# The last unit's inverses and normalization, issued inside the first layer's steps

## The chip, the cores and the metric

The kernel runs on one core of a Trainium2 chip. The metric is the device time in microseconds (us) of one execution. The engines work side by side, each through its own list of instructions in order, and they meet at semaphores: TensorE (PE, its weight loads are PEld), VectorE (DVE), ScalarE (ACT), GpSimd (POOL), and SyncE (SP), which issues nearly all DMAs of this kernel.

## What is computed

Linear attention over 4 batches of 8 heads (576 positions, head size 64), then two feed-forward layers over the 2304 tokens. Cut to what matters:

```python
proj = x @ w_phi                               # for q and for k, 64 -> 128 features
proj = proj - max(abs(proj))                   # per row
phi = concat([exp(proj), exp(-proj)])
kv = phi(k).T @ v ; z = sum(phi(k))
num = phi(q) @ kv ; den = phi(q) @ z + 1e-6
attn = num / den                               # 32 heads -> x of 2304 x 512
h = x @ w_in1 ; x = (h * cos(h)) @ w_out1      # 512 -> 2048 -> 512
h = x @ w_in2 ; out = (max(h, 0) ** 2) @ w_out2
```

The feed-forward weights are float64. Every matmul of the two layers is made of three, of high and low halves.

## The kernel before

**Attention.** The heads are taken two at a time: 16 units, u = 0 to 15, four for each batch. A unit is cut into named steps, and a planner puts the steps of all units, of the first weight tiles' conversion and of the start of the first layer into one list (`keys`), which `emit` then issues one by one. Each engine carries out its own instructions in the order in which the list names them. The last steps of a unit are a chain over several engines. `C` copies numerators and denominators out of PSUM into the tile `tm` (ACT). `D1` reshapes the 2 x 576 denominators from `tm` into `cp` of 32 x 36 (two small DMAs on SP's queue). `I` adds 1e-6 and takes the reciprocal (two DVE instructions, L613 and L614). `D3` writes `cp` to `db` in DRAM, and `D4` reads it back, spread over 64 partitions a head, into `dn` (three DMAs on SP's queue). `Z0` and `Z1` multiply `tm` by `dn` into `xbuf`, the layers' input (two POOL instructions, L629).

**Feed-forward.** `feed_forward` goes through ten blocks j of tokens: j = 0 to 4 for the first layer (tokens 0 to 511, 512 to 767, then three blocks of 512), j = 5 to 9 for the second. A block has 16 chunks c of the hidden size. At step i of a block PE runs `G1(j, i)`, twelve matmuls (L289 to L291), and `G2(j, i - 3)`, twelve matmuls (L385) that use the result of `G1` three steps earlier. Between them stands the elementwise chain of a chunk: `A1` on ACT (L304, L305), `A2a` and `A2b` on DVE (L309, L311), `B1` on ACT (L314, L315), `B2` on DVE (L319), `B3` on ACT, which writes the high half of `g` (L324), and `B4` on DVE, which writes the low half (L327). Here g(c) is what `G2` of chunk c needs. There are two buffers for `tr` and two for `g`. `G1` of the chunks 0 to 3 of block 0, and parts of their elementwise work, are steps of the list `keys` and stand before `feed_forward`.

**Weights.** 32 tiles of the first layer are loaded as float64 and turned into two halves on the chip: three ACT instructions (L227, L229, L231), four on DVE or POOL (L242, L244, L246, L249), one on ACT (L255) and one more (L259). Tiles 0 to 19 are done in `keys`. Tiles 20 to 31 are converted on ACT and DVE inside block 0, about nine tiles in ten steps. Their loads are issued on SP's queue in two groups: tiles 20 to 28 (`wnext`, nine loads of 512 KB) when the attention's buffers are free, and tiles 29 to 31 (`wlast`, three loads) when `tm`, `cp` and `dn` are.

**The order at the seam.** The last lines of the kernel issue `keys` up to the last attention step that is not a tail step, then the nine `wnext` loads, then the rest of `keys`, then the three `wlast` loads, then `feed_forward`. The rest of `keys` holds, among the early elementwise steps of chunks 0 to 3, the tail of unit 15: `C01`, `C11`, `D1`, `I`, `D3`, `D4`, `Z0`, `Z1`. Unit 15 holds tokens 1728 to 2303, which the first layer reads in its blocks 3 and 4.

Of the kernel before, what the change touches and what calls it, by code (L numbers as in the profile page):

```python
# [158 lines left out]
def attention_ffn_kernel(  # L159
# [20 lines left out]
    NU = len(UNITS)  # L180
    NEARLY, NNEXT = 21, 9
# [5 lines left out]
    with tc.manual_schedule():  # L187
        const = ctx.enter_context(tc.tile_pool(name="const", bufs=1))
        pools_w = [ctx.enter_context(tc.tile_pool(name="wearly", bufs=1))]
# [18 lines left out]
        NTILE = len(order)  # L208
        weights, raw_t, mag_t = {}, {}, {}

        def w_slot(i, dtype, shape, name):
            pool = pools_w[(i >= NEARLY) + (i >= NEARLY + NNEXT)]
            return pool.tile(shape, dtype, tag=f"w{i}", name=name)

        def w_load(layer, n):
            part, c = order[n]
            s = w_slot(n + 1 - layer, I32, [P, KDM * P, 2], "raw")
            src = ((w_in1, w_out1), (w_in2, w_out2))[layer][part]
            nc.sync.dma_start(out=s.rearrange("p f t -> p (f t)"), in_=src.bitcast(I32)[c * P:(c + 1) * P, :])
            raw_t[layer, n] = s  # L220
# [49 lines left out]
        def split_x(j, kk, part):  # L270
            _, o, n = BLOCKS[j]
            src = xbuf[:, kk, o:o + n]
            x = work(XS[kk][part], [P, n], F32R, "xs")
            if part == 0:
                nc.scalar.activation(out=x, in_=src, func=ACTF.Copy)
                xs_t[kk] = (x,)
            else:
                hi = xs_t[kk][0]
                nc.vector.tensor_tensor(out=x, in0=src, in1=f(hi), op=ALU.subtract)
                xs_t[kk] = (hi, x)  # L280

        def G1(j, c):
            layer, _, n = BLOCKS[j]
            hps = bank(H_BANKS[c % 4], name="h")[:, 0:n]
            w = weights[layer, 0, c]
            ih, il = (w[:, i].rearrange("p (k f) -> p k f", k=KDM) for i in range(2))
            for kk in range(KDM):
                xh, xl = xs_t[kk]
                nc.tensor.matmul(out=hps, lhsT=ih[:, kk, :], rhs=xh, start=kk == 0, stop=False)  # L289
                nc.tensor.matmul(out=hps, lhsT=ih[:, kk, :], rhs=xl, start=False, stop=False)  # L290
                nc.tensor.matmul(out=hps, lhsT=il[:, kk, :], rhs=xh, start=False, stop=kk == KDM - 1)  # L291
            h_t[c] = hps
# [37 lines left out]
        def elementwise(j, i, conv):  # L330

            layer = BLOCKS[j][0]

            def a(name):
                if i < KFF:
                    part(name, j, i)

            def b(name):
                if 1 <= i <= KFF:
                    part(name, j, i - 1)  # L340

            if layer == 0:
                b("B1")
                conv(w_join, 0)
                a("A1")
                b("B2")
                conv(w_join, 1)
                a("A2a")
                conv(w_join, 2)
                conv(w_join, 3)  # L350
            else:
                conv(w_join, 0)
                a("A1")
                conv(w_join, 1)
                b("B1")
                conv(w_join, 2)
                conv(w_join, 3)
            b("B3")
            if layer == 0:
                a("A2b")  # L360
            conv(w_split, 0)
            b("B4")
            conv(w_split, 1)
            for step in range(3):
                conv(w_words, step)

        def G2(j, c):
            layer, _, n = BLOCKS[j]
            g = g_t.pop(c)
            gh, gl = g[:, 0], g[:, 1]  # L370
            w = weights[layer, 1, c]
            oh, ol = w[:, 0], w[:, 1]
            na = KDM if layer == 0 else n // P
            if c == 0:
                acc[:] = [bank(ACC_BANKS[m], name=f"acc{m}") for m in range(na)]
            for m in range(na):
                sl = slice(m * P, (m + 1) * P)
                if layer == 0:
                    trip = ((oh[:, sl], gh), (oh[:, sl], gl), (ol[:, sl], gh))
                    o = acc[m][:, 0:n]  # L380
                else:
                    trip = ((gh[:, sl], oh), (gl[:, sl], oh), (gh[:, sl], ol))
                    o = acc[m]
                for i, (l, r) in enumerate(trip):
                    nc.tensor.matmul(out=o, lhsT=l, rhs=r, start=c == 0 and i == 0, stop=c == KFF - 1 and i == 2)  # L385

        def evict(j):
            layer, o, n = BLOCKS[j]
            for m, a in enumerate(acc):
                if layer == 0:  # L390
                    dst, src = xbuf[:, m, o:o + n], a[:, 0:n]
                else:
                    dst, src = mag_p.tile([P, DM], F32, tag="mag", name="ot"), a
                if m % 2:
                    nc.scalar.activation(out=dst, in_=src, func=ACTF.Copy)
                else:
                    nc.vector.tensor_copy(dst, src)
                if layer == 1:
                    nc.sync.dma_start(out=out[o + m * P:o + (m + 1) * P, :], in_=dst)
# [4 lines left out]
        class Ticks:  # L404
# [16 lines left out]
            def share(self, rate):  # L421
                self.due += rate
                n = int(self.due)
                self.due -= n
                return [self.tick() for _ in range(n)]
# [12 lines left out]
        def retire(j, i):  # L438
            if j == LAST_0:
                for n, (p, c) in enumerate(order):  # L440
                    if c + LA * p == i:
                        w_load(1, n)

        def feed_forward():
            for j in range(len(BLOCKS)):
                for i in range(KFF + LA):
                    if i < KFF and ("G1", j, i) not in early:
                        G1(j, i)
                    now = share(j, i)
                    elementwise(j, i, now[0] if now else lambda fn, *a: None)  # L450
                    for conv in now[1:]:
                        for fn, *a in STAGES:
                            conv(fn, *a)
                    if i == KFF and j + 1 < len(BLOCKS):
                        for kk in range(KDM):
                            split_x(j + 1, kk, 0)
                            split_x(j + 1, kk, 1)
                    if i >= LA:
                        G2(j, i - LA)
                    retire(j, i)  # L460
                evict(j)


        lctx = ExitStack()
        lp = lctx.enter_context(tc.tile_pool(name="lp", bufs=2, side="right"))
        dp = lctx.enter_context(tc.tile_pool(name="dp", bufs=2, space=bass.MemoryType.DRAM))
        with ExitStack() as actx:
# [25 lines left out]
            def rouse(n):  # L493

                o = bank("nm")
                for _ in range(n):
                    nc.tensor.matmul(out=o, lhsT=zeros[:, 0:P], rhs=zeros[:, P:], start=True, stop=True)
# [146 lines left out]
            for u in range(NU):  # L644
# [27 lines left out]
                for half in range(2):  # L672
                    for h in range(2):
                        n, tiles = f"{h}{half}", [("nm", h, half)]
# [46 lines left out]
            keys = arrange(steps)  # L721
            behind = max(i for i, key in enumerate(keys) if key[0] in STEPS and key[0] not in ("C01", "C11", "D1", "I", "D3", "D4", "Z0", "Z1"))

            def emit(keys):
                for key in keys:
                    fn, *a = run[key]
                    fn(*a)
                    early.add((key[0], 0, key[1]))
                    if key == ("PJt", 0):
                        rouse(4)  # L730
# [3 lines left out]
        pools_w.append(ctx.enter_context(tc.tile_pool(name="wnext", bufs=1)))  # L734
        for n in range(NEARLY - 1, NEARLY - 1 + NNEXT):
            w_load(0, n)
        emit(keys[behind + 1:])
        lctx.close()
        pools_w.append(ctx.enter_context(tc.tile_pool(name="wlast", bufs=1)))
        for n in range(NEARLY - 1 + NNEXT, NTILE):  # L740
            w_load(0, n)
        feed_forward()


# [54 lines left out]
```

## Time and profile before

| | |
|---|---|
| median of 3 runs | 1002.8 us (1002.77 to 1004.1) |
| profiled execution, its own time | 1002.51 us |
| its span in the profile | 1000.6 us |
| PE busy | 980.8 us, 98% |
| ACT busy | 626.0 us, 63% |
| DVE busy | 551.3 us, 55% |
| POOL busy | 124.1 us, 12% |

The span is the time between the first and the last instruction of the profiled execution, and its own time is 1.9 us longer. A busy share is an average over the whole span. Attention and the first weights take about the first 205 us, the two layers the rest. The page also cuts the span into 40 slices of 25 us: PE shows 9 tenths in 37 of them, 6 in the ninth (200 to 225 us), 8 in the tenth and 8 in the last. TensorE's granted clock shows 8 in the ninth and the tenth slice, and 9 (that is 90% of full speed or more) in all others.

### The profile page before, as it was taken

To read this page: it belongs to the slowest core of one execution; us is meant where nothing else is said; L and a number is where in the kernel's file an instruction comes from. 1 tells how busy PE (TensorE), PEld (TensorE's weight loads), DVE (VectorE), ACT (ScalarE), POOL (GpSimd) and SP (SyncE) were. 2 spreads that over 40 slices of the span, in tenths; PEclk is the share of its full clock that TensorE was granted. 3 is DMA by queue.
4 is the path that set the end of the run, shared out by engine and by line. 5 is a ranking of instruction groups with operands and counts; after the bars stand their busy time and mean duration, and the time that the engine had idled before them with its cause. 6 is when DMAs were issued, how large, how long until landed. Compare 5 with 4: busy or idle time off the path is not lost.

```text
span 1000.6 us, 14041 instructions
## 1 busy us (share of the span) xinstructions
PE 980.8 (98%) x5305; PEld 834.0 (83%) x5305; DVE 551.3 (55%) x944; ACT 626.0 (63%) x1213; POOL 124.1 (12%) x98
## 2 busy tenths in 40 slices
PE   9999999968999999999999999999999999999998
PEld 8988899857889988888888888888888888888897
DVE  5798878649876564555558888984112111211211
ACT  4888788659867665565559888995334333433343
POOL 0567777510000000000000000000000000000000
PEclk9999999988999999999999999999999999999999
DMA  6566642151000000000016661001000100100010
GB/s 223 180 206 218 191 122 74 37 202 64 1 1 1 2 1 0 1 1 1 1 43 191 194 198 49 1 1 43 1 1 0 43 1 1 43 1 1 0 44 22
DMA packets 23284, 60.01 MB, mean 60 GB/s; under 512 B 4400, under 2 KB 4528, under 8 KB 23216
## 3 DMA queue, kind: packets, MB, share of 16 engines
q1 hardware_dynamic: 23072, 59.04, 18.2%
q8 instruction: 42, 0.69, 0.3%
q14 instruction: 26, 0.21, 0.1%
q10 hardware_dynamic: 144, 0.07, 0.0%
HBM read 54.23 MB, written 4.79 MB: 59 GB/s over the span
## 4 chain that ended last, share of the span: by engine, by line
PE 91%; DMA 3%; ACT 2%; DVE 2%; POOL 1%; issue 1%; SPq 0%; DVEq 0%; POOLq 0%
PE acc L385 39%; PE h L291 13%; PE h L290 13%; PE h L289 13%; PE nm L591 5%; PE kv L544 5%; PE pj L510 2%; PE tp L572 1%; DMA db<-cp 1%; DMA cp<-tm 1%; DMA dn<-db 1%; DMA raw<-in_dram 1%; PE kv L552 1%; PE pj L519 1%; ACT eq L583 0%
## 5 line engine op out<-in xcount | busy, mean ns | idle before, releaser
L327 DVE TENSOR_TENSOR g<-tr,g 128x512 fp32r<-128x512 f32 (+1 forms) x160 | 101.8, 636 | 274.6 <-ACT g L324 273.7
L289 PE MATMUL h<-xs,w 128*128 128x512 f32 (+1 forms) x640 | 235.9, 369 | 0.0
L291 PE MATMUL h<-xs,w 128*128 128x512 f32 (+1 forms) x640 | 235.5, 368 | 0.0
L290 PE MATMUL h<-xs,w 128*128 128x512 f32 (+1 forms) x640 | 235.4, 368 | 0.0
L385 PE MATMUL acc<-g,w 128*128 128x512 f32 (+1 forms) x960 | 210.4, 371 | 11.4 <-ACT g L324 7.2
L385 PE MATMUL acc<-w,g 128*128 128x512 f32 x864 | 206.7, 389 | 0.0
L385 PEld LDWEIGHTS acc<-g,w 128*128 128x128 f32 x960 | 169.5, 190 | 42.8 <-ACT g L324 7.6
L385 PEld LDWEIGHTS acc<-w,g 128*128 128x128 f32 x864 | 161.3, 188 | 32.9
L324 ACT ACTIVATE g<-tr 128x512 fp32r<-128x512 f32 (+1 forms) x160 | 94.1, 588 | 128.9 <-PE acc L385 96.6
L289 PEld LDWEIGHTS h<-xs,w 128*128 128x128 f32 x640 | 120.6, 188 | 20.6
L290 PEld LDWEIGHTS h<-xs,w 128*128 128x128 f32 x640 | 120.6, 188 | 20.6
L291 PEld LDWEIGHTS h<-xs,w 128*128 128x128 f32 x640 | 120.7, 189 | 20.0
L307 ACT ACTIVATE tr<-h 128x512 f32<-128x512 f32 (+1 forms) x80 | 44.2, 553 | 103.5 <-PE h L291 102.4
L309 DVE SCALAR_TENSOR_TENSOR tr<-tr,h 128x512 f32<-128x512 f32 (+1 forms) x80 | 50.7, 634 | 62.8 <-ACT tr L305 60.9
L319 DVE SCALAR_TENSOR_TENSOR tr<-tr,h 128x512 f32<-128x512 f32 (+1 forms) x80 | 50.7, 634 | 41.8 <-ACT tr L315 40.9
L591 PE MATMUL nm<-eq,ks 128*128 128x288 f32 x256 | 70.8, 410 | 0.1
L314 ACT ACTIVATE tr<-tr 128x512 f32<-128x512 f32 (+1 forms) x80 | 46.8, 585 | 35.2 <-DVE tr L311 35.1
L304 ACT ACTIVATE tr<-h 128x512 f32<-128x512 f32 (+1 forms) x80 | 43.6, 545 | 31.6 <-PE h L291 29.6
L544 PEld LDWEIGHTS kv<-v,e 128*128 128x128 f32 x512 | 59.8, 192 | 1.8
L544 PE MATMUL kv<-v,e 128*128 128x65 f32 x512 | 59.2, 273 | 0.0
L525 DVE TENSOR_REDUCE m<-pj 128x4 f32<-128x512 f32 (+1 forms) x80 | 49.4, 618 | 8.1 <-PE pj L510 8.1
L583 ACT ACTIVATE eq<-tp 128x512 f32<-128x512 f32 (+1 forms) x96 | 41.8, 491 | 17.8 <-PE tp L572 17.5
(55 smaller groups left out, 1060.9 us busy)
## 6 DMA issues: line engine op xcount, KB each, us to landing
raw<-in_dram SPq DMA_DIRECT2D x64, 512.0 KB, 3.8
kq<-in_dram SPq DMA_DIRECT2D x16, 384.0 KB, 3.8
v<-in_dram SPq DMA_DIRECT2D x16, 330.0 KB, 5.1
dn<-db SPq DMA_DIRECT2D x32, 144.0 KB, 3.0
out_dram<-ot SPq DMA_DIRECT2D x18, 256.0 KB, 3.0
kq<-in_dram SPq DMA_DIRECT2D x16, 256.0 KB, 3.7
cp<-tm SPq DMA_DIRECT2D x32, 2.2 KB, 2.4
db<-cp SPq DMA_DIRECT2D x16, 4.5 KB, 4.2
```

Source lines behind the costliest of these rows:

```text
L289: nc.tensor.matmul(out=hps, lhsT=ih[:, kk, :], rhs=xh, start=kk == 0, stop=False)
L290: nc.tensor.matmul(out=hps, lhsT=ih[:, kk, :], rhs=xl, start=False, stop=False)
L291: nc.tensor.matmul(out=hps, lhsT=il[:, kk, :], rhs=xh, start=False, stop=kk == KDM - 1)
L309: nc.vector.scalar_tensor_tensor(out=r, in0=t, scalar=-C1, in1=h_t[c], op0=ALU.mult, op1=ALU.add)
L314: nc.scalar.activation(out=r, in_=r, func=ACTF.Sin, scale=0.5)
L319: nc.vector.scalar_tensor_tensor(out=t, in0=r, scalar=1.0, in1=h_t.pop(c), op0=ALU.subtract, op1=ALU.mult, reverse0=True)
L324: nc.scalar.activation(out=g[:, 0], in_=t, func=ACTF.Copy)
L327: nc.vector.tensor_tensor(out=g[:, 1], in0=t, in1=f(g[:, 0]), op=ALU.subtract)
L385: nc.tensor.matmul(out=o, lhsT=l, rhs=r, start=c == 0 and i == 0, stop=c == KFF - 1 and i == 2)
L525: nc.vector.tensor_reduce(out=m[:, 0:n], in_=pj[:, 0:n, :], axis=AX.X, op=ALU.max, apply_absolute_value=True)
L544: nc.tensor.matmul(out=acc[:, s, h, 0:D + 1], lhsT=e[:, t, s, :], rhs=v_t[u][:, t, h, 0:D + 1], start=t == 0 and h == 0 and s == 0, stop=F ...
L591: nc.tensor.matmul(out=nm[:, 0:SH], lhsT=ks_t[u][:, s, 2 * h:2 * h + 2, :].rearrange("p a d -> p (a d)"), rhs=eq_t[u][:, h, s, half * SH:( ...
```

## The change

The five steps `I`, `D3`, `D4`, `Z0` and `Z1` of unit 15 are taken out of the list and issued by a function that `feed_forward` calls at the end of step i = 6 of block 0. The close of the pool that holds `tm`, `cp` and `dn`, and the three `wlast` loads, go with them. `D1` stays where it was.

```diff
-        def feed_forward():
+        def feed_forward(between):
...
                     retire(j, i)
+                    if (j, i) in between:
+                        between[j, i]()
                 evict(j)
...
-        emit(keys[behind + 1:])
-        lctx.close()
-        pools_w.append(ctx.enter_context(tc.tile_pool(name="wlast", bufs=1)))
-        for n in range(NEARLY - 1 + NNEXT, NTILE):
-            w_load(0, n)
-        feed_forward()
+        deferred = [(n, NU - 1) for n in ("I", "D3", "D4", "Z0", "Z1")]
+        emit([key for key in keys[behind + 1:] if key not in deferred])
+
+        def normalize_last():
+            emit(deferred)
+            lctx.close()
+            pools_w.append(ctx.enter_context(tc.tile_pool(name="wlast", bufs=1)))
+            for n in range(NEARLY - 1 + NNEXT, NTILE):
+                w_load(0, n)
+
+        feed_forward({(0, 6): normalize_last})
```

Only DVE's order differs. On DVE, at the start of block 0 before the change, the two instructions of `I` for unit 15 (tile `cp_2489`) stand behind the low halves of g(0) and g(1) (L327) and ahead of the first DVE steps of chunks 2 and 3 (tiles `tr_2512` and `tr_2518`):

```order
L327 TENSOR_TENSOR g_2493<-tr_2421,g_2493 128x512
L327 TENSOR_TENSOR g_2510<-tr_2434,g_2510 128x512
L613 TENSOR_SCALAR cp_2489<-cp_2489 32x36
L614 RECIPROCAL cp_2489<-cp_2489 32x36
L309 SCALAR_TENSOR_TENSOR tr_2512<-tr_2512,h_2471 128x512
L311 SCALAR_TENSOR_TENSOR tr_2512<-tr_2512 128x512
L309 SCALAR_TENSOR_TENSOR tr_2518<-tr_2518,h_2497 128x512
```

The same place on DVE after the change (chunk 3's tile is now called `tr_2516`):

```order
L327 TENSOR_TENSOR g_2493<-tr_2421,g_2493 128x512
L327 TENSOR_TENSOR g_2510<-tr_2434,g_2510 128x512
L309 SCALAR_TENSOR_TENSOR tr_2512<-tr_2512,h_2471 128x512
L311 SCALAR_TENSOR_TENSOR tr_2512<-tr_2512 128x512
L309 SCALAR_TENSOR_TENSOR tr_2516<-tr_2516,h_2497 128x512
```

Chunk 2's first step now stands directly behind g(1). The second place is on DVE at the end of step 6 of block 0, after the change: the low half of g(5) (L327), the last conversion of weight tile 23 (L259), the moved pair (L615 and L616 by the changed file's lines), and the start of step 7.

```order
L311 SCALAR_TENSOR_TENSOR tr_2678<-tr_2678 128x512
L327 TENSOR_TENSOR g_2686<-tr_2631,g_2686 128x512
L259 TENSOR_TENSOR w_2689<-mag_2599,w_2689 128x512
L615 TENSOR_SCALAR cp_2489<-cp_2489 32x36
L616 RECIPROCAL cp_2489<-cp_2489 32x36
L242 TENSOR_SCALAR mag_2693<-mag_2693 128x512
L319 SCALAR_TENSOR_TENSOR tr_2678<-tr_2678,h_2662 128x512
```

The pair stands 42 rows later than it did. On SP the DMAs of unit 15 (`cp`, `db`, `dn`) still stand between the nine and the three weight loads, and POOL's list still ends with unit 15's two multiplications: what changes there is only when the semaphores let them start.

## Rows read from the trace of the kernel before

**Rows 1.** The page's first part: busy us, share of the span, instructions.

```profile
PE 980.8 (98%) x5305; PEld 834.0 (83%) x5305; DVE 551.3 (55%) x944; ACT 626.0 (63%) x1213; POOL 124.1 (12%) x98
```

**Rows 2.** Waits, 205 to 233 us: who waited for whom, us, times, longest.

```profile
ACT tr L314 <- DVE tr L311: 10.1, 1, 10.1
DVE cp L613 <- DMA cp<-tm: 10.0, 1, 10.0
```

**Rows 3.** The chain that ended last, around 207 us: start us, us, what.

```profile
207.61 7.87 DMA cp<-tm
```

**Rows 4.** Timeline of PE, 205 to 234 us: start, us, line, [idle before <-releaser].

```profile
205.76 2.88 PE L385 MATMUL acc<-g,w 128*128 128x512 f32 x12
208.48 0.39 PE L289 MATMUL h<-xs,w 128*128 128x512 f32 x1
...
216.41 0.39 PE L291 MATMUL h<-xs,w 128*128 128x512 f32 x1
223.98 0.80 PE L385 MATMUL acc<-g,w 128*128 128x512 f32 x1 [7.18 <-ACT g L324]
228.68 4.58 PE L385 MATMUL acc<-g,w 128*128 128x512 f32 x11 [3.90 <-DVE g L327]
233.09 0.39 PE L289 MATMUL h<-xs,w 128*128 128x512 f32 x1
```

**Rows 5.** Windows of 1 us: each engine's busy us, then PEclk, DMA share, GB/s.

```profile
218.00:219.00 1.00, 0.00 (x0) 0.00 (x0) 0.93 (x3) 0.94 (x3) 0.00 (x0) 0.94 0.00 0
219.00:220.00 1.00, 0.00 (x0) 0.00 (x0) 0.50 (x1) 0.97 (x2) 0.00 (x0) 0.50 0.29 81
```

**Rows 6.** Timeline of DVE, 215 to 230 us.

```profile
215.61 0.17 DVE L613 TENSOR_SCALAR cp<-cp 32x36 f32<-32x36 f32 x1 [9.98 <-DMA cp<-tm]
...
216.11 0.62 DVE L309 SCALAR_TENSOR_TENSOR tr<-tr,h 128x512 f32<-128x512 f32 x1
...
222.67 1.71 DVE L249 TENSOR_TENSOR mag<-mag,raw 128x512 f32<-128x512 f32 x1
224.31 1.63 DVE L242 TENSOR_SCALAR mag<-mag 128x512 f32<-128x512 f32 x1
...
227.33 0.69 DVE L249 TENSOR_TENSOR mag<-mag,raw 128x512 f32<-128x512 f32 x1
227.94 0.68 DVE L327 TENSOR_TENSOR g<-tr,g 128x512 fp32r<-128x512 f32 x1
...
229.14 0.42 DVE L242 TENSOR_SCALAR mag<-mag 128x512 f32<-128x512 f32 x1
```

**Rows 7.** Timelines of ACT, POOL and SP, 205 to 227 us.

```profile
205.57 0.63 ACT L305 ACTIVATE tr<-tr 128x512 f32<-128x512 f32 x1
...
206.72 0.63 ACT L305 ACTIVATE tr<-tr 128x512 f32<-128x512 f32 x1
...
221.93 3.71 POOL L629 TENSOR_TENSOR xbuf<-tm,dn 64x576 f32<-64x576 f32 x2 [21.80 <-DMA dn<-db]
...
225.67 1.29 SPq L219 DMA_DIRECT2D raw<-in_dram  x3
```

**Rows 8.** The weight loads (tile raw), 200 to 300 us: from issue to landing.

```profile
DMA to landing us min/median/max: 3.5/6.4/10.3
```

**Rows 9.** Timelines of DVE and ACT, 232 to 292 us, single instructions of block 0.

```profile
232.54 0.68 DVE L327 TENSOR_TENSOR g<-tr,g 128x512 fp32r<-128x512 f32 x1
...
253.09 0.69 DVE L327 TENSOR_TENSOR g<-tr,g 128x512 fp32r<-128x512 f32 x1
...
257.02 0.69 DVE L327 TENSOR_TENSOR g<-tr,g 128x512 fp32r<-128x512 f32 x1
...
267.01 0.67 ACT L227 ACTIVATE mag<-raw 128x512 f32<-128x512 f32 x1
...
284.60 0.69 DVE L327 TENSOR_TENSOR g<-tr,g 128x512 fp32r<-128x512 f32 x1
...
291.54 0.69 DVE L327 TENSOR_TENSOR g<-tr,g 128x512 fp32r<-128x512 f32 x1 [0.76 <-ACT g L324]
```

## The prediction

> **What bounds the kernel now.** The page's first part comes first: PE is busy 98% of the span, the next engine 63% [rows 1]. So time is won only where PE stands idle or runs slowly, and the page's slices show one such place, the ninth and tenth, 200 to 250 us. The waits of that stretch name two long ones besides PE's own: DVE's L613 waited 10.0 us for the DMA into `cp`, and ACT's L314 waited 10.1 us for DVE's L311 [rows 2]. The reader is to see one line of dependence in them. The pair `I` of unit 15 stands in DVE's list ahead of the elementwise work of chunk 2. Its DMA was issued at 207.61 us, behind nine weight loads, and took 7.87 us, to 215.48 [rows 3]. DVE started the pair at 215.61 after 9.98 us idle [rows 6]; so it had been free at 205.63. Everything that ACT and DVE do for g(2) came after that.
>
> PE's timeline shows the price. A step of PE is `G1` and `G2`, 2.72 us each (205.76 to 208.48 [rows 4]), so 5.44 us. The last matmul of `G1(5)` began at 216.41; one matmul takes 2.72 / 12 = 0.23 us, so `G2(2)` could have begun at 216.64 and `G1(6)` at 219.36. `G2(2)` began at 223.98, when ACT had written the high half of g(2), stopped again until 228.68, when DVE had written the low half, and `G1(6)` began at 233.09 [rows 4]. The loss is 233.09 - 219.36 = **13.73 us**: 7.34 us before the first matmul, 3.90 us before the second, and 2.49 us because the twelve took 0.80 + 4.41 us in place of 2.72. They were slow because the granted clock had left its upper level: the window 218 to 219 us shows 0.94 and the next 0.50 [rows 5], that is 1.2 GHz in place of 2.4 from about 218.9 us, 2.2 us after PE ran dry.
>
> **The change part by part.** *The pair leaves its place.* DVE, free at 205.63, next needs ACT's L305 of chunk 2, which ended at 205.57 + 0.63 = 206.20 [rows 7]. So L309, which began at 216.11 [rows 6], begins at about 206.23: 9.88 us earlier. Chunk 3's L305 ended at 207.35 [rows 7], before DVE comes to it, and the first weight loads landed 3.5 to 10.3 us after their issue [rows 8] in a queue that was done by 215.48 with the small DMA behind it; ACT and DVE come to tile 20 only after two chunks' work, at about 210 us, when the first of the nine has long landed. So all of this work moves by 9.88 us.
>
> *POOL's two multiplications leave too.* They ran from 221.93 for 3.71 us [rows 7], and in that time DVE's L249 took 1.71 us and L242 1.63 us, where the same lines take 0.69 and 0.42 us a little later [rows 6]. I read that as DVE held up by POOL for 1.02 + 1.21 = 2.23 us. At the old place this hold is gone, so g(2), ready at 227.94 + 0.68 = 228.62 [rows 6], is ready at 228.62 - 9.88 - 2.23 = 216.51. PE wants its low half for the second matmul, at 216.87. The margin is 0.36 us: no stall, but narrowly.
>
> *From there on DVE's lead over PE decides.* g(3) was ready at 232.54 + 0.68 [rows 9], so it is now at 221.11; PE wants it one step on, at 222.31: lead 1.20 us. DVE needs (253.09 - 232.54) / 4 = 5.14 us a step [rows 9], PE 5.44, so the lead grows by 0.30 a step, to 2.10 at g(6).
>
> *The pair at its new place* comes at about 231.9 us (230.71 for the low half of g(5), two instructions of 0.6 us more), 16 us after its DMA landed: no wait. It costs DVE 216.11 - 215.61 = 0.50 us [rows 6]: lead 1.60 at g(6), 1.90 at g(7).
>
> *The multiplications at their new place* start as long after the pair as before, 221.93 - 215.61 = 6.32 us, so from 238.2 to 241.9 us, in a stretch where DVE has no idle time, ahead of g(7). Call the hold h. The nearest row is the hold of this very pair, 2.23 us; the bounds are nothing, and the whole 3.71 us. I take 2.23: DVE's list there is the same sort of work. It passes the lead at g(7) by 0.33 us, and PE stalls for that.
>
> *What is left at the block's end.* After g(7) comes the step without a conversion, 257.02 - 253.09 = 3.93 us [rows 9], which gives 1.51 us of lead; four steps more give 1.20: lead 2.71 at g(12). Then `G1` has run out and PE asks for g(13), g(14) and g(15) 2.72 us apart, 8.16 us in all, while DVE needs 5.14 + (291.54 - 284.60) = 12.08 us for them [rows 9]: 3.92 us of lead are used up, 1.21 too many, a second stall. Without any hold the lead at g(12) would be 4.61 and nothing would stall. So the two stalls together are h - 0.69, and nothing below that: 1.54 us for h = 2.23, 3.02 for 3.71. Both are shorter than the 2.2 us after which the clock fell, so I cost no slow matmuls.
>
> *The three late loads* left 10.06 us after the pair (225.67 [rows 7]), so now at 242.0, and land 3.5 to 10.3 us later [rows 8], by 252.3. ACT's first use of tile 29 was at 267.01 [rows 9]; moved with PE, at 253.3. Nothing; the cover is at least 1.0 us. `D3` and `D4` on SP are ahead of nothing but these loads. The products in `xbuf` are read in blocks 3 and 4, some 100 us on.
>
> **The sum.** 13.73 - 1.54 = 12.19 us gained. The profiled execution took 1002.51 us: 990.3. The median of the runs is 0.29 us above that execution: **990.6 us**, 1.2% less.
>
> At this place the Trainium skill, *SBUF — State Buffer*, section "SBUF: two separate sides", speaks against the change: it says that VectorE and GpSimd share one pair of ports as an exclusive lock, and that who starts first keeps it for a whole instruction while the other is fully blocked. The two long DVE rows agree in kind, since the first of them ends only when one multiplication has. By the rule a DVE without gaps would lose nearly the whole of both multiplications, and the sum would be near 992 us.
>
> **The rivals.**
> *POOL's hold is full.* If each multiplication stops DVE until it is over, DVE runs on for at most one instruction, 0 to 0.6 us, into each: h = 2.5 to 3.7, stalls 1.8 to 3.0, time 990.9 to 992.1 us. For it: DVE has no gaps there; against it: the one hold of this pair was 2.23, also between busy rows.
> *No hold that counts.* If h stays below 0.69 us, all 13.73 us come back: 1002.8 - 13.7 = 989.1 us. For it: several DVE instructions of a step read PSUM or wait for ACT; against it, the same two rows.
> *A stall long enough for the clock.* The margin at g(2) is 0.36 us. If g(2) comes more than 2.6 us late, for a load or a hold that I have not seen, PE is idle past the 2.2 us and pays the slow matmuls again: at least 2.3 + 2.5 = 4.8 us on top, 994 to 997 us. Nothing in the rows asks for it.
> *The other side, slower.* The three late loads could come after ACT wants tile 29: ACT would stand at L227 with the elementwise work behind it, as DVE stood before. To end slower than before by over 0.2%, ACT must be held 12.2 + 2.0 = 14.2 us, so the loads must land at 267.5 us, 15 us after the latest time worked out. Only a chain of `I`, `D3`, `D4`, `Z` that took 25 us in place of 10 would do it.
> *No change.* Another wait could stand behind the pair and hold DVE just as long. Against it: ACT's result for chunk 2 was there 0.57 us after DVE was free.
>
> **How the numbers follow.** The forecast 0.45, full hold 0.20, no hold 0.20, a stall with the clock 0.10, slower 0.03, no change 0.02. A difference of 0.2%, 2.0 us, is about what a measurement of this kernel can tell from none. The first four cases are all faster by more than that: 0.95; the same 0.02; slower 0.03. The range goes from just under the case without a hold, 988.6, past the full hold, 992.1, to 993.2, which takes in a late g(2) that does not reach the clock; the first three cases hold 0.85.
>
> **What would show it.** In the new profile: DVE's L309 of chunk 2 at about 206.2 us with no wait for `cp`; `G2(2)` near 216.7 and `G1(6)` near 219.4 us; the granted clock at its upper level through 200 to 250 us; the pair near 232 us without a wait; POOL's multiplications from about 238 us with one or two DVE instructions of over 1 us beside them; PE stalls of some tenths near 244 us and about 1 us near 275 to 280 us, in the last four `G2` of block 0; ACT's L227 of tile 29 without a wait for its load. The prediction is wrong if PE stalls at `G2(2)` again, if the clock falls after it, or if ACT waits for the three late loads.

## The result, and the profile after

The changed kernel takes 988.75 us (median of 4 runs, 988.64 to 990.6) against 1002.78 us before (4 runs, 1002.31 to 1004.1): the ratio is 0.9862, 95% interval 0.9845 to 0.9879. It is faster by 14.0 us where 12.2 were forecast.

The page's first part, and its slices of 25 us for PE and the granted clock:

```profile
PE 977.4 (99%) x5305; PEld 831.9 (84%) x5305; DVE 548.8 (56%) x944; ACT 625.6 (63%) x1213; POOL 123.3 (12%) x98
...
PE   9999999999999999999999999999999999999998
...
PEclk9999999999999999999999999999999999999999
```

The hole of the ninth and tenth slice is gone. What TensorE still waited for from 205 to 300 us, and what POOL did (who waited for whom, us, times, longest):

```profile
POOL xbuf L631 <- DMA dn<-db: 37.2, 1, 37.2
...
PE acc L385 <- DVE g L327: 0.8, 2, 0.5
```

The 10.0 and 10.1 us of [rows 2] are not in the list any more. POOL's 37.2 us cost nothing: it has no other work. Of PE's 0.8 us 0.49 stand in block 0 (the row at 276.35 below), the rest behind it. PE's timeline, the rows that answer to [rows 4]:

```profile
204.76 2.88 PE L385 MATMUL acc<-g,w 128*128 128x512 f32 x12
...
215.64 2.88 PE L385 MATMUL acc<-g,w 128*128 128x512 f32 x12
218.36 0.39 PE L289 MATMUL h<-xs,w 128*128 128x512 f32 x1
...
276.35 0.96 PE L385 MATMUL acc<-g,w 128*128 128x512 f32 x3 [0.49 <-DVE g L327]
...
281.92 0.28 PE L289 MATMUL h<-xs,w 128*128 128x256 f32 x1
```

`G2(0)` begins at 204.76, `G2(2)` at 215.64, two steps of 5.44 us later and without a wait, `G1(6)` at 218.36. A good measure for all that follows is the length of block 0, from the first matmul of `G2(0)` to the first matmul of block 1. After the change it is 281.92 - 204.76 = **77.16 us**. Before, the first matmul of block 1 began at 295.67:

```profile
295.67 0.28 PE L289 MATMUL h<-xs,w 128*128 128x256 f32 x1
```

With 205.76 from [rows 4] that is 89.91 us. Without the loss of 13.73 us it would be 76.18. So block 0 is 12.75 us shorter, and 0.98 us of TensorE's stalls are left. The two profiled executions (1002.51 and 988.67 us) differ by 13.84 us. Of the 1.09 us that block 0 does not explain, 1.00 us lies ahead of `G2(0)`, in code that is the same in both; over the seven profiled executions of this study `G2(0)` began between 204.38 and 207.15 us.

DVE's timeline, with the rows that answer to [rows 6] and the new place of the pair:

```profile
205.23 0.69 DVE L309 SCALAR_TENSOR_TENSOR tr<-tr,h 128x512 f32<-128x512 f32 x1 [0.60 <-ACT tr L305]
...
214.89 0.68 DVE L327 TENSOR_TENSOR g<-tr,g 128x512 fp32r<-128x512 f32 x1
...
224.63 0.68 DVE L327 TENSOR_TENSOR g<-tr,g 128x512 fp32r<-128x512 f32 x1
...
229.76 0.68 DVE L327 TENSOR_TENSOR g<-tr,g 128x512 fp32r<-128x512 f32 x1
...
230.97 0.17 DVE L615 TENSOR_SCALAR cp<-cp 32x36 f32<-32x36 f32 x1
...
235.19 0.68 DVE L327 TENSOR_TENSOR g<-tr,g 128x512 fp32r<-128x512 f32 x1
...
236.39 1.66 DVE L242 TENSOR_SCALAR mag<-mag 128x512 f32<-128x512 f32 x1
237.97 0.68 DVE L319 SCALAR_TENSOR_TENSOR tr<-tr,h 128x512 f32<-128x512 f32 x1
238.57 1.05 DVE L244 TENSOR_SCALAR mag<-mag 128x512 int32<-128x512 int32 x1
...
242.07 0.69 DVE L327 TENSOR_TENSOR g<-tr,g 128x512 fp32r<-128x512 f32 x1
```

DVE waits 0.60 us for ACT in place of 9.98 for the DMA. The pair, at 230.97, waits for nothing. Beside POOL's two multiplications two conversion instructions are long, 1.66 and 1.05 us, where they take 0.42 alone; L319 between them is not. POOL's multiplications, the three late loads and ACT's first instruction on tile 29 (single rows of three timelines), and the loads' time to landing from 200 to 300 us:

```profile
236.30 3.04 POOL L631 TENSOR_TENSOR xbuf<-tm,dn 64x576 f32<-64x576 f32 x2 [37.17 <-DMA dn<-db]
...
239.37 1.46 SPq L219 DMA_DIRECT2D raw<-in_dram  x3
...
254.65 0.65 ACT L227 ACTIVATE mag<-raw 128x512 f32<-128x512 f32 x1
...
DMA to landing us min/median/max: 3.5/6.5/10.5
```

ACT found tile 29 landed: its row has no wait.

### The profile page after: what moved, and what is told of

The parts are those of the page before. It is cut to its first block, busy times and chain, and to the rows that moved or that the text cites. A ratio compares the mean times of both kernels' runs of the same rounds, so it can differ in the third digit from the quotient of the medians.

```text
span 986.9 us, 14043 instructions
## 1 busy us (share of the span) xinstructions
PE 977.4 (99%) x5305; PEld 831.9 (84%) x5305; DVE 548.8 (56%) x944; ACT 625.6 (63%) x1213; POOL 123.3 (12%) x98
## 4 chain that ended last, share of the span: by engine, by line
PE 85%; DVE 5%; ACT 4%; DMA 2%; issue 2%; POOL 1%; SPq 0%; DVEq 0%; POOLq 0%
PE acc L385 36%; PE h L291 12%; PE h L290 12%; PE h L289 12%; PE nm L593 4%; PE kv L546 4%; PE pj L512 2%; PE tp L574 1%; DVE tr L311 1%; DMA db<-cp 1%; DMA dn<-db 1%; ACT tr L305 1%; DVE w L259 1%; ACT tr L304 1%; DVE mag L246 1%
## 5 line engine op out<-in xcount | busy, mean ns | idle before, releaser
L327 DVE TENSOR_TENSOR g<-tr,g 128x512 fp32r<-128x512 f32 (+1 forms) x160 | 101.8, 636 | 275.0 <-ACT g L324 274.0
L319 DVE SCALAR_TENSOR_TENSOR tr<-tr,h 128x512 f32<-128x512 f32 (+1 forms) x80 | 50.6, 633 | 40.4 <-ACT tr L315 39.8
L631 POOL TENSOR_TENSOR xbuf<-tm,dn 64x576 f32<-64x576 f32 x32 | 45.6, 1426 | 62.4 <-DMA dn<-db 61.2
```

The costliest lines, as they stand in the source:

```text
L319: nc.vector.scalar_tensor_tensor(out=t, in0=r, scalar=1.0, in1=h_t.pop(c), op0=ALU.subtract, op1=ALU.mult, reverse0=True)
L327: nc.vector.tensor_tensor(out=g[:, 1], in0=t, in1=f(g[:, 0]), op=ALU.subtract)
```

## The experiments

**D1 ahead of the loads.** The kernel before, with one thing changed: SP issues the two small DMAs of `D1` ahead of the nine weight loads. The pair keeps its old place in DVE's list.

```diff
-        for n in range(NEARLY - 1, NEARLY - 1 + NNEXT):
-            w_load(0, n)
-        emit(keys[behind + 1:])
+        rest = keys[behind + 1:]
+        at = rest.index(("D1", NU - 1)) + 1
+        emit(rest[:at])
...
+        emit(rest[at:])
```

> The kernel before, with the two small DMAs of D1 for unit 15 issued ahead of the nine weight loads in place of behind them; the pair I keeps its old place in VectorE's list. The measure is the length of block 0, from the first matmul of G2(0) to the first matmul of block 1: 89.91 us before, 77.16 after the change, 76.18 without any stall. Theory A (VectorE's wait for the DMA into cp is the whole cause; the list's order matters only through it): the pair waits under 1 us, block 0 takes 76.5 to 78.5 us, the whole about 988.5 to 991 us. Rival B (what counts is that the pair and POOL's multiplications no longer stand ahead of g(2), by their work and POOL's hold): most of the loss stays, block 0 over 85 us, the whole over 997 us.

Measured: 987.94 us (987.25 to 991.21), ratio to before 0.987 (0.9851 to 0.9888). DVE's and PE's timelines, and the small DMAs' time to landing (tile cp, 200 to 215 us):

```profile
204.91 0.16 DVE L613 TENSOR_SCALAR cp<-cp 32x36 f32<-32x36 f32 x1
...
222.00 1.15 DVE L244 TENSOR_SCALAR mag<-mag 128x512 int32<-128x512 int32 x1
...
223.66 1.32 DVE L246 CUSTOM_DVE_ANT_0 mag<-raw,mag 128x1024 uint16<-128x1024 uint16 x1
...
205.13 2.88 PE L385 MATMUL acc<-g,w 128*128 128x512 f32 x12
...
281.45 0.28 PE L289 MATMUL h<-xs,w 128*128 128x256 f32 x1
...
DMA to landing us min/median/max: 1.6/1.6/9.9
```

The DMAs into `cp` land in 1.6 us in place of 7.87 [rows 3], the pair at its old place waits for nothing, and block 0 takes 76.32 us. (The 9.9 us are those of `D3`, which now stands behind the loads; no engine but POOL waits for what follows it.) POOL's hold, at 222 to 225 us and so behind g(3) and ahead of g(4), was 1.36 us (L244 and L246 are long; alone they take 0.42 and 0.69), and 0.14 us of stall are left: 0.84 us less than after the change, where the hold is 0.51 us longer and the pair takes about 0.3 us of DVE's lead (both are worked out below). Theory A holds: VectorE's instructions need not move at all. The wait of the pair for its DMA, which stood behind nine loads, was the root of the loss. The hold ahead of g(2), which B names, was a part of the loss and went with the wait: without the wait DVE was done with g(2) at 215.93 us, and POOL's multiplications began at 221.43.

**D1 behind five loads.** The same edit, with five of the nine loads ahead of `D1` and four behind it.

> The kernel before, with D1 of unit 15 issued behind five of the nine weight loads, in place of behind all nine; the pair I keeps its old place. Theory A (the wait is as long as the loads ahead of D1 take, and TensorE pays it behind a margin of about 0.4 us): the DMA lands near 210 us (in the time of the kernel before), the pair waits about 4.5 us in place of 9.98, g(2) is about 4.4 us late and TensorE stands for about 4 us in two pieces of some 2 us each. If the granted clock does not fall in them, block 0 takes about 80.3 us; if it falls, up to 2.5 us more, 82.8. Rival B (the wait does not go with the number of loads, a fixed latency of the small DMA at this place): block 0 near 89.9 us, as before, or 76.3, as with D1 ahead of all loads.

Measured: 998.05 us (995.68 to 998.25), ratio to before 0.9942 (0.9922 to 0.9962). DVE's timeline, then PE's:

```profile
210.69 0.17 DVE L613 TENSOR_SCALAR cp<-cp 32x36 f32<-32x36 f32 x1 [5.60 <-DMA cp<-tm]
...
220.18 1.80 DVE L249 TENSOR_TENSOR mag<-mag,raw 128x512 f32<-128x512 f32 x1
221.90 1.88 DVE L327 TENSOR_TENSOR g<-tr,g 128x512 fp32r<-128x512 f32 x1
```

```profile
219.11 0.51 PE L385 MATMUL acc<-g,w 128*128 128x512 f32 x1 [2.85 <-ACT g L324]
223.84 4.81 PE L385 MATMUL acc<-g,w 128*128 128x512 f32 x11 [4.22 <-DVE g L327]
...
291.07 0.28 PE L289 MATMUL h<-xs,w 128*128 128x256 f32 x1
```

`G2(0)` began at 205.22 here, so block 0 took 85.85 us: between none and nine, as A says, but 3 us more than my upper figure. The wait was 5.60 us and not 4.5, and I had left out that POOL's multiplications still stand ahead of g(2) in this kernel: L249 and L327 were held for 1.11 and 1.20 us. The low half of g(2) was ready at 223.78, 7.45 us after PE wanted it (216.33): 5.60 us of wait and 2.31 of hold, less a margin of 0.46. So the two are paid one behind the other. The other 2.2 us of the 9.67 by which block 0 exceeds 76.18 are slow matmuls: the granted clock fell here too.

How the wait goes with the loads is less simple than A has it. The chain that ended last, around 203 us (window 196 to 250), has the second small DMA (start us, us, what):

```profile
203.40 7.17 DMA cp<-tm
```

Behind nine loads it took 7.87 us [rows 3]. It landed 4.91 us earlier here, and 4.21 us of that is that SP issued it earlier; from issue to landing it took nearly as long behind five loads as behind nine. Why is not shown.

**The multiplications twice.** The changed kernel, with `Z0` and `Z1` of unit 15 carried out twice (the second pair writes the same values).

```diff
-            emit(deferred)
+            emit(deferred + deferred[-2:])
```

> The changed kernel, with POOL's two multiplications of unit 15 carried out twice (the second time they write the same values), so that POOL holds VectorE for about twice as long. Theory A (VectorE's lead over TensorE is small, and beyond about 0.7 us every us of hold becomes a stall of TensorE): hold 3.3 to 4.5 us in place of 1.87, block 0 77.16 + 1.4 to 2.6 = 78.6 to 79.8 us, the whole about 990 to 991.5 us. Rival B (the lead is larger than I worked out, and the stall of about 1 us at the end of block 0 has nothing to do with POOL): block 0 stays at 77.0 to 77.4 us.

Measured: 990.82 us (989.16 to 992.77), ratio to before 0.9892 (0.9877 to 0.9907). DVE's timeline beside POOL's 6.74 us, and PE's:

```profile
238.78 1.66 DVE L242 TENSOR_SCALAR mag<-mag 128x512 f32<-128x512 f32 x1
...
240.96 1.05 DVE L244 TENSOR_SCALAR mag<-mag 128x512 int32<-128x512 int32 x1
...
242.54 1.33 DVE L246 CUSTOM_DVE_ANT_0 mag<-raw,mag 128x1024 uint16<-128x1024 uint16 x1
243.90 1.80 DVE L249 TENSOR_TENSOR mag<-mag,raw 128x512 f32<-128x512 f32 x1
```

```profile
207.15 2.88 PE L385 MATMUL acc<-g,w 128*128 128x512 f32 x12
...
286.02 0.28 PE L289 MATMUL h<-xs,w 128*128 128x256 f32 x1
```

Taken alone the four take 0.42, 0.42, 0.69 and 0.69 us, so the hold is 5.84 - 2.22 = 3.62 us, against 1.66 + 1.05 - 0.84 = 1.87 after the change. Block 0 takes 78.87 us. The stalls went from 0.98 to 2.69 us, 1.71 us for 1.75 us of hold: A holds.

**Step 7 in place of step 6.** The changed kernel with `{(0, 7): normalize_last}`: POOL's multiplications fall into the step that has no conversion.

> The changed kernel, with the five steps and the three late loads issued at the end of step 7 in place of step 6, so that POOL's multiplications fall into step 9, which has no weight conversion: VectorE there has waits for ScalarE of 0.16 and 0.46 us, and only two of its four instructions read two operands from SBUF. Theory A: the hold is smaller, 0.5 to 1.3 us, block 0 takes 76.2 to 76.9 us, and the loads still land before ScalarE wants them (248.5 against 254.7 us). Rival B (the stall at the end of block 0 is independent of the hold): block 0 stays at 77.0 to 77.4 us. The whole differs from the changed kernel's by less than 1 us by either theory.

Measured: 989.22 us (987.92 to 990.61), ratio to before 0.9876 (0.9861 to 0.9892). The one long DVE instruction beside POOL's work, and PE:

```profile
243.80 1.32 DVE L311 SCALAR_TENSOR_TENSOR tr<-tr 128x512 f32<-128x512 f32 x1
```

```profile
204.93 2.88 PE L385 MATMUL acc<-g,w 128*128 128x512 f32 x12
...
281.09 0.28 PE L289 MATMUL h<-xs,w 128*128 128x256 f32 x1
```

The hold is 1.32 - 0.69 = 0.63 us and block 0 takes 76.16 us, all that there was to win in it. That is at the lower end of A's 76.2 to 76.9 us. B falls: the stall at the block's end goes with the hold. The whole does not show it, since its runs lie up to 2.7 us apart.

**Step 9.** The changed kernel with `{(0, 9): normalize_last}`.

> The changed kernel, with the five steps and the three late loads issued at the end of step 9 of block 0 in place of step 6. Theory A: the loads are issued at about 255 us, land from 258.5 us on, and ScalarE, which wants tile 29 at 254.7 us, waits about 4 us for the first of them; the lead of some 3 to 4 us is used up and TensorE stalls by 3 to 5 us in all: block 0 79 to 81.5 us, the whole 990.5 to 993 us. Rival B (the place among the steps does not matter as long as it is behind g(2)): block 0 77.0 to 77.4 us, the whole as after the change.

Measured: 991.8 us (990.67 to 993.29), ratio to before 0.9904 (0.989 to 0.9918). Waits from 203 to 296 us, then two rows of DVE's timeline, then PE:

```profile
PE acc L385 <- DVE g L327: 2.8, 3, 1.6
...
ACT mag L227 <- DMA raw<-in_dram: 2.0, 1, 2.0
```

```profile
249.32 1.93 DVE L259 TENSOR_TENSOR w<-mag,w 128x512 fp32r<-128x512 f32 x1
251.17 1.65 DVE L242 TENSOR_SCALAR mag<-mag 128x512 f32<-128x512 f32 x1
```

```profile
204.38 2.88 PE L385 MATMUL acc<-g,w 128*128 128x512 f32 x12
...
283.82 0.28 PE L289 MATMUL h<-xs,w 128*128 128x256 f32 x1
```

ACT now waits for tile 29, 2.0 us where I expected 4 (the loads left at 252.57 us and not at 255, since neither the pair nor a hold stood ahead of the end of step 9), and block 0 takes 79.44 us. So the cover of the three late loads, which the forecast put at 1.0 us or more, is used up between step 7, where no engine waited for them, and step 9. But POOL's hold is longer here as well, 1.24 + 1.23 = 2.47 us in the two rows of DVE. Of the 3.26 us of stalls about 1.6 would be the hold's by the slope of the other runs (hold less 0.9 us), which leaves about 1.7 us for the late loads: an estimate, since no run has the late loads without the hold. The rival of the slower side is a real mechanism with a small price here.

## Why the prediction was right

**The loss and its cause.** 13.73 us were read from PE's timeline, and block 0 without any stall came out at 76.16 us in one experiment, where 89.91 - 13.73 is 76.18. The cause is shown from both sides: with the pair moved, and with its DMA moved.

**The margin at g(2).** Forecast 0.36 us; g(2) was ready at 214.89 + 0.68 = 215.57, wanted at 215.64 + 0.23 = 215.87: 0.30 us.

**The hold.** This is the term that was mis-sized: 2.23 us forecast, 1.87 measured. Besides, the pair took less of DVE's lead than the 0.50 us forecast: from g(5) to g(6), with the pair between, DVE took 235.19 - 229.76 = 5.43 us, and 229.76 - 224.63 = 5.13 us the step before, so 0.30 us. DVE's lead at g(7) was just positive: ready at 242.07 + 0.69 = 242.76, wanted at 215.87 + 5 x 5.44 = 243.07, 0.31 us, where the forecast had it 0.33 us short, and the stall near 244 us did not come. At the block's end it did, at 276.35. The rule "stalls are the hold less 0.69 us" gives 1.18 us; measured 0.98 with a hold of 1.87, 2.69 with 3.62, nothing with 0.63. The slope is right; what is free is about 0.9 us, and the 0.2 us more are those that the pair did not take.

**The full hold, the rival that the Trainium skill stood behind.** Not seen: 1.87 us of POOL's 3.04. The working missed a condition that the Trainium skill states, *SBUF — State Buffer*, section "Who interferes with whom": a VectorE instruction with at most one SBUF input, outside the two-port modes, does not contend with GpSimd. The trace agrees: L319, whose other operand is in PSUM, took its usual 0.68 us at 237.97, inside POOL's 236.30 to 239.34, between two instructions that were held. The section of the Trainium skill that the prediction names also ties the lock to VectorE instructions in a two-port mode or with two SBUF inputs, so the 992 us of the forecast did not follow from it.

**The sum.** In block 0 12.75 us came back where 12.19 were forecast. The rest of the 14.0 is mainly the start of the executions (1.00 us between the profiled ones), which no step of the change explains. That the whole gained more than 12.75 us is chance as far as these runs show.

**What the forecast costed at nothing** stayed so: a wait of the pair at its new place, the DMAs, and the three late loads at step 6.

## What to carry to other kernels

An instruction that waits for a DMA holds up everything behind it on its engine (9.98 us on DVE here), so look for the one whose DMA was issued behind a batch of large loads: either let it stand later, or issue its small DMA ahead of the batch; the whole times do not tell the two apart here (988.75 and 987.94 us), and block 0 took 77.16 and 76.32 us. When work is moved into a stretch that has no gaps, count how far the feeding engine is ahead of the one that it feeds, and spend that lead on the extra work; what goes beyond it is paid nearly one for one (1.71 us for 1.75 here). A place without such work in the loop (here the step without a conversion) took it for nothing.

## What the runs showed of the hardware

The granted clock did not fall after a fixed time of idleness. Before, it fell to 0.50, that is 1.2 GHz, about 2.2 us after PE ran dry [rows 5]. With D1 behind five loads PE stood for 2.85 us until 219.11, and the clock stayed at 1.00; after one matmul it stood again, and only then the clock fell (windows of 1 us: each engine's busy us, then PEclk, DMA share, GB/s):

```profile
218.00:219.00 1.00, 0.00 (x0) 0.00 (x0) 0.96 (x3) 1.00 (x3) 0.00 (x0) 1.00 0.71 207
...
221.00:222.00 1.00, 0.00 (x0) 0.00 (x0) 1.00 (x2) 0.26 (x1) 0.93 (x2) 0.70 0.00 0
222.00:223.00 1.00, 0.00 (x0) 0.00 (x0) 1.00 (x1) 0.00 (x0) 1.00 (x1) 0.50 0.00 0
```

So the sentence of the forecast that stalls under 2.2 us keep the clock was true of these stalls, but 2.2 us is no bound.
